# Looping over head pairs outermost, and contracting the mode weights by quarters of d

## The chip, the core and the metric

The kernel runs on one core of a Trainium2 chip. A time is the device time of one execution in microseconds (us). The engines are named as in the profile: PE is TensorE (matmul), PEld its weight loads, DVE is VectorE, ACT is ScalarE, POOL is GpSimd and SP is SyncE. POOL and SP issue the loads and stores (DMA) here. Matmuls leave their results in PSUM; the copy that takes one out to SBUF is called its eviction. The granted clock (PEclk, or the number before the DMA share in a window) is the share of PE's full clock that the profile's record shows.

## The reference, cut to what matters

Eight batches, eight heads, 576 positions, 64 elements per head, so d = 512. A causal attention with a decay that is a difference of cumulative sums is followed by a mixing in frequency space.

```python
scores = q @ k.T / sqrt(64)
cum    = cumsum(log(clip(f, 1e-4, 1)))
scores = where(causal, -1e9, scores + cum[i] - cum[j])
x      = softmax(scores) @ v              # joined to [8, 576, 512]

X  = rfft(x, axis=1)[:, :64]              # 64 modes
Yr = Xr @ w_r - Xi @ w_i                  # w_r, w_i: [64, 512, 512]
Yi = Xr @ w_i + Xi @ w_r
y  = irfft(Y, n=576, axis=1)
u  = x + y
return u + relu(u @ w_ch)                 # w_ch: [512, 512]
```

The weights of the modes are 2 x 64 x 1.05 MB = 134 MB in float32. They are converted to bf16 on their way into SBUF, where they are 67 MB. All of q, k and v is 28 MB in float32, or 14.2 MB in bf16. The transform of x along the sequence treats every column of x by itself, and the contraction with the weights is a sum over d. Both facts are what the change lives on.

## The kernel before

Attention loops over batches, and over the four head pairs of a batch inside. A pair's scores have their 64 head elements on 64 partitions. The decay of a key enters as the bias of the exp, so every tile of 128 keys and every head needs an exp of its own.

```python
pairs = [(b, g) for b in range(B) for g in range(H // 2)]
for i, (b, g) in enumerate(pairs):
    # ... loads of a new batch, transposes of the next pair, AV of the last batch
    emit_qk_pair(b, g, [])

# in emit_qk_pair
for hp in range(2):
    bp = hp * 64
    nc.tensor.matmul(pscore[:Mj, 0:n],
        lhsT=KTs[bp : bp + 64, s0 : s0 + Mj],
        rhs=QTs[bp : bp + 64, s0 + c0 : s0 + c0 + n], start=True, stop=True)
# ...
nc.scalar.activation(et[:Mj, c0 : c0 + n], pss[hp][:Mj, 0:n], ACT.Exp,
                     bias=biasAll[:Mj, jb, bh : bh + 1], scale=scale)
```

AV multiplies the exps with V, which carries a column of ones for the sum of the softmax. After all ten AV groups of a batch, the batch is transformed (`emit_dft_batch`). Only when the last batch is transformed can the contraction with the weights start: a mode takes all 512 rows of d, four matmuls deep in PSUM.

```python
wpool = ctx.enter_context(tc.tile_pool(name="wpool", bufs=6))
# ... all attention ...
for m in range(NM):
    wb = wpool.tile([128, 2, NEB, D], BF16, tag="wb", name="wb")
    nc.gpsimd.dma_start(wb[:, 0], moe_w_r[m].rearrange("(dc p) e -> p dc e", p=128))
    nc.gpsimd.dma_start(wb[:, 1], moe_w_i[m].rearrange("(dc p) e -> p dc e", p=128))
    A = psM.tile([128, 2, NEB, 2 * B], F32, tag="A", name="A")
    for t in range(2):
        for ebx in range(NEB):
            for dc in range(NEB):
                nc.tensor.matmul(A[:, t, ebx, :],
                    lhsT=wb[:, t, dc, ebx * 128 : (ebx + 1) * 128],
                    rhs=_strided(XT[:, dc, 0, m, 0:1], [[1, 2], [NM * 2, B]]),
                    start=(dc == 0), stop=(dc == NEB - 1))
    # ... ACT copies A, DVE forms Yr and Yi ...
    if m % 8 == 3:
        xw_for_batch(m // 8)          # x @ w_ch of one batch, "XW" below
# ... tail: y = irfft, y @ w_ch, u, relu, store: 40 blocks of 128 or 64 rows
```

The softmax here doesn't subtract the row's maximum and nothing guards it: scores larger than these inputs give would overflow.

Of the kernel before, what the change touches and what calls it, by code (L numbers as in the profile page):

```python
# [21 lines left out]
def kernel(  # L24
# [19 lines left out]
    NEB = D // 128  # L44
    BH = B * H
    scale = 1.0 / math.sqrt(Dh)

    const = ctx.enter_context(tc.tile_pool(name="const", bufs=1))
    xpool = ctx.enter_context(tc.tile_pool(name="xpool", bufs=1))
    wpool = ctx.enter_context(tc.tile_pool(name="wpool", bufs=6))  # L50

    x_all = xpool.tile([128, B, NSB, D], BF16, name="x_all")
    XT = xpool.tile([128, NEB, B, NM, 2], BF16, name="XT")
# [4 lines left out]
    masks.make_identity(nc, ident_bf[:])  # L58
    masks.make_identity(nc, ident_f[:])
    masks.make_upper_triangular(nc, trimask[:], val=1.0, diag=True)  # L60

    iota_p_i = const.tile([128, 1], I32, name="iota_p_i")
    nc.gpsimd.iota(iota_p_i[:], pattern=[[0, 1]], base=0, channel_multiplier=1)
    s_i = const.tile([128, NSB], I32, name="s_i")
    nc.gpsimd.iota(s_i[:], pattern=[[128, NSB]], base=0, channel_multiplier=1)
    s_f = const.tile([128, NSB], F32, name="s_f")
    nc.vector.tensor_copy(s_f[:], s_i[:])
    nc.vector.tensor_scalar(s_f[:], s_f[:], float(S - 1), None, ALU.min)
    ones_row = const.tile([1, 128], F32, name="ones_row")
    nc.vector.memset(ones_row[:], 1.0)  # L70
    negpi = const.tile([128, 1], F32, name="negpi")
    nc.vector.memset(negpi[:], -math.pi)

    bas = const.tile([128, NSB, NM, 2], BF16, name="bas")
    BI = const.tile([128, S], BF16, name="BI")
    cumT = const.tile([128, NSB, BH], F32, name="cumT")
    biasAll = const.tile([128, NSB, BH], F32, name="biasAll")
    wch = const.tile([128, NEB, D], BF16, name="wch")

    TWO_PI_OVER_S = 2.0 * math.pi / S  # L80

    with ExitStack() as sctx:
        ps_setup = sctx.enter_context(
            tc.tile_pool(name="ps_setup", bufs=2, space=bass.MemoryType.PSUM)
        )
        ssb = sctx.enter_context(tc.tile_pool(name="setup_sb", bufs=1))

        gem = ssb.tile([128, NSB], F32, name="gem")
        nc.vector.tensor_scalar(gem[:], s_f[:], 432.0, None, ALU.is_ge)
        spl = ssb.tile([128, NSB], F32, name="spl")  # L90
        nc.vector.tensor_scalar(spl[:], s_f[:], 144.0, None, ALU.add)
        sz = ssb.tile([128, NSB], F32, name="sz")
        nc.vector.scalar_tensor_tensor(
            sz[:], gem[:], -float(S), spl[:], ALU.mult, ALU.add
        )
        S0 = ssb.tile([128, NSB], F32, name="S0")
        C0 = ssb.tile([128, NSB], F32, name="C0")
        nc.scalar.activation(
            S0[:], s_f[:], ACT.Sin, bias=negpi[:, :], scale=TWO_PI_OVER_S
        )  # L100
        nc.scalar.activation(
            C0[:], sz[:], ACT.Sin, bias=negpi[:, :], scale=TWO_PI_OVER_S
        )
        Zt = ssb.tile([128, NSB, NM, 2], F32, name="Zt")
        nc.vector.memset(Zt[:, :, 0, 0], 1.0)
        nc.vector.memset(Zt[:, :, 0, 1], 0.0)
        nc.vector.tensor_scalar(Zt[:, :, 1, 0], C0[:], -1.0, None, ALU.mult)
        nc.vector.tensor_copy(Zt[:, :, 1, 1], S0[:])
        wrot = ssb.tile([128, NSB, 2], F32, name="wrot")
        nc.vector.tensor_copy(wrot[:, :, :], Zt[:, :, 1, :])  # L110
        ta = ssb.tile([128, NSB, 32], F32, name="ta")
        tb = ssb.tile([128, NSB, 32], F32, name="tb")
        M = 2
        while M < NM:
            wr = wrot[:, :, 0]
            wi = wrot[:, :, 1]
            t0 = ssb.tile([128, NSB], F32, name="t0")
            t1 = ssb.tile([128, NSB], F32, name="t1")
            nc.vector.tensor_tensor(t0[:], wr, wr, ALU.mult)
            nc.vector.tensor_tensor(t1[:], wi, wi, ALU.mult)  # L120
            t2 = ssb.tile([128, NSB], F32, name="t2")
            nc.vector.tensor_tensor(t2[:], wr, wi, ALU.mult)
            nc.vector.tensor_tensor(wrot[:, :, 0], t0[:], t1[:], ALU.subtract)
            nc.vector.tensor_scalar(wrot[:, :, 1], t2[:], 2.0, None, ALU.mult)
            Are = Zt[:, :, 0:M, 0]
            Aim = Zt[:, :, 0:M, 1]
            wr_b = _strided(wrot[:, :, 0:1], [[2, NSB], [0, M]])
            wi_b = _strided(wrot[:, :, 1:2], [[2, NSB], [0, M]])
            nc.vector.tensor_tensor(ta[:, :, 0:M], Are, wr_b, ALU.mult)
            nc.vector.tensor_tensor(tb[:, :, 0:M], Aim, wi_b, ALU.mult)  # L130
            nc.vector.tensor_tensor(Zt[:, :, M : 2 * M, 0], ta[:, :, 0:M], tb[:, :, 0:M], ALU.subtract)
            nc.vector.tensor_tensor(ta[:, :, 0:M], Are, wi_b, ALU.mult)
            nc.vector.tensor_tensor(tb[:, :, 0:M], Aim, wr_b, ALU.mult)
            nc.vector.tensor_tensor(Zt[:, :, M : 2 * M, 1], ta[:, :, 0:M], tb[:, :, 0:M], ALU.add)
            M *= 2
        nc.vector.tensor_copy(bas[:, :, :, :], Zt[:, :, :, :])
        coef = ssb.tile([128, 1], F32, name="coef")
        nc.vector.memset(coef[:], 2.0 / S)
        nc.vector.memset(coef[0:2, :], 1.0 / S)
        for sc in range(NSB):  # L140
            ns = SBLK[sc]
            bip = ps_setup.tile([128, 128], F32, tag="sps", name="bip")
            nc.tensor.transpose(
                bip[:, :ns],
                Zt[:ns, sc, :, :].rearrange("p m ri -> p (m ri)"),
                ident_f[:ns, :ns],
            )
            nc.vector.tensor_scalar(  # L148
                BI[:, sc * 128 : sc * 128 + ns], bip[:, :ns], coef[:], None, ALU.mult
            )  # L150

        ft = ssb.tile([BH, S], F32, name="ft")
        nc.sync.dma_start(ft[:], f.rearrange("b h s -> (b h) s"))
        lf = ssb.tile([BH, S], F32, name="lf")
        nc.scalar.activation(lf[:], ft[:], ACT.Ln)
        onesS = ssb.tile([BH, S], F32, name="onesS")
        nc.vector.memset(onesS[:], 1.0)
        cum = ssb.tile([BH, S], F32, name="cum")
        nc.vector.tensor_tensor_scan(
            cum[:], onesS[:], lf[:], 0.0, ALU.mult, ALU.add  # L160
        )
        cum_ps = ps_setup.tile([128, NSB, BH], F32, tag="sps2", name="cum_ps")
        for sc in range(NSB):
            ns = SBLK[sc]
            nc.tensor.transpose(
                cum_ps[:ns, sc, :],
                cum[:, sc * 128 : sc * 128 + ns],
                ident_f[:BH, :BH],
            )
        nc.vector.tensor_copy(cumT[:, 0:4, :], cum_ps[:, 0:4, :])  # L170
        nc.vector.tensor_copy(cumT[:64, 4, :], cum_ps[:64, 4, :])
        nc.vector.memset(cumT[64:128, 4, :], 0.0)
        R_ps = ps_setup.tile([128, BH], F32, tag="sps2", name="R_ps")
        nc.tensor.matmul(
            R_ps[:],
            lhsT=ones_row[0:1, :],
            rhs=cumT[0:1, 2, :],
            start=True,
            stop=True,
        )  # L180
        Rb = ssb.tile([128, BH], F32, name="Rb")
        nc.vector.tensor_copy(Rb[:], R_ps[:])
        nc.vector.tensor_tensor(
            biasAll[:, :, :],
            _strided(Rb[:, :], [[0, NSB], [1, BH]]),
            cumT[:, :, :],
            ALU.subtract,
        )

        wch_f = ssb.tile([128, NEB, D], F32, name="wch_f")  # L190
        nc.sync.dma_start(
            wch_f[:], moe_w_ch.rearrange("(eb p) e -> p eb e", p=128)
        )
        nc.vector.tensor_copy(wch[:], wch_f[:])

    with ExitStack() as actx:
        qkbf = actx.enter_context(tc.tile_pool(name="qkbf", bufs=2))
        vapool = actx.enter_context(tc.tile_pool(name="vapool", bufs=2))
        qtkt = actx.enter_context(tc.tile_pool(name="qtkt", bufs=2))
        epool = actx.enter_context(tc.tile_pool(name="epool", bufs=14))  # L200
        psA = actx.enter_context(
            tc.tile_pool(name="psA", bufs=4, space=bass.MemoryType.PSUM)
        )
        psB = actx.enter_context(
            tc.tile_pool(name="psB", bufs=2, space=bass.MemoryType.PSUM)
        )
        psT = actx.enter_context(
# [195 lines left out]
        for it in tails:  # L403
            it()
# [168 lines left out]
```

## Time and profile before

The kernel took 671.9 us (median of 4 runs, 670.98 to 673.73). These are the lines of its page that matter: the span, the busy tenths of PE in 40 slices of 16.8 us, the GB/s that the DMA engines moved in the same slices (bytes as they are written, so bf16 for the weights), and the chain of waits that ended last, by engine and by line.

```profile
span 671.5 us, 10980 instructions
...
PE   0169999999999999999888895222222222225996
...
GB/s 199 185 148 150 36 120 9 98 9 99 8 100 11 97 10 26 1 1 58 202 207 206 207 206 206 206 206 206 206 206 206 206 206 207 206 206 81 134 247 184
...
PE 45%; DMA 44%; DVE 5%; issue 3%; POOL 2%; ACT 0%; SPq 0%; POOLq 0%; DVEq 0%; ACTq 0%
DMA wb<-in_moe_w_r_dram 38%; PE pav L328 14%; PE pscore L293 11%; PE QTp L249 3%; PE KTp L256 3%; DMA wb<-in_moe_w_i_dram 3%; PE px L351 3%; PE pu L507 1%; PE pyw L480 1%; PE pz L529 1%; PE pu L514 1%; PE pz L522 1%; DVE x_all L337 1%; DMA qb<-in_q_dram 1%; PE pxw L435 1%
```

Read the two rows of slices under each other, counted from one. From the 4th to the 19th slice PE is full and the DMA moves 1 to 150 GB/s. From the 20th to the 36th the DMA moves 202 to 207 GB/s in every slice; PE has XW to do in the first five of them, and then two tenths. Then PE is full again. These are three stages with different limits, and they hardly overlap. The Trainium skill, "Perfetto Trace Analysis", section Optimization Strategy, says of such kernels that interleaving the regimes may pay; that is the plan of this change.

| stage | us | limit |
|---|---|---|
| attention | 34 to 310 | PE |
| contraction of the modes, XW in between | 320 to 612 | weight loads |
| tail | 614 to 671 | PE |

The table of windows says the same with numbers. Its columns are the window, its length, busy time and instructions of each engine, the granted clock of PE, the DMA share and the GB/s.

```profile
core 0: us, PE busy (x) PEld busy (x) DVE busy (x) ACT busy (x) POOL busy (x), PEclk, DMA share, GB/s
34.00:310.00 276.00, 262.49 (x1732) 131.67 (x1731) 121.97 (x568) 163.39 (x384) 91.71 (x111) 0.81 0.82 56
320.00:612.00 292.00, 129.73 (x2197) 86.65 (x2195) 38.28 (x146) 38.68 (x99) 80.00 (x108) 0.62 1.24 205
28.00:38.00 10.00, 2.29 (x8) 0.83 (x8) 0.00 (x0) 0.00 (x0) 9.60 (x12) 1.00 2.42 154
```

PE is busy 262.5 of 276 us in the first stage and 130 of 292 us in the second. The third window is a stretch at the start in which only q, k and v are loaded: 154 GB/s, against 206 GB/s for the weights. The rows of q, k and v in HBM are 256 bytes long. What PE waits for in the second stage is in the view of waits (total us, times, longest):

```profile
PE A L456 <- DMA wb<-in_moe_w_i_dram: 85.2, 49, 2.7
PE A L456 <- DMA wb<-in_moe_w_r_dram: 78.0, 48, 2.0
```

That is 163 us of waiting for weights. A stage that is so clearly limited by loads would be free if its loads ran under attention.

PE is not working at its peak in the first stage. This stretch of PE's timeline (start, us, engine, line, operation, shapes) has AV matmuls (`pav`) with 128 rows and a score (`pscore`) with 64 rows.

```profile
260.67 0.25 PE L328 MATMUL pav<-vaug,et_3067 128*64 128x65 bf16 x1
260.73 0.25 PE L328 MATMUL pav<-vaug,et_3068 128*64 128x65 bf16 x1
260.91 0.34 PE L293 MATMUL pscore<-QTs,KTs 64*128 64x192 bf16 x1
261.18 0.26 PE L328 MATMUL pav<-vaug,et_3069 128*64 128x65 bf16 x1
```

The `pav` start 0.06 us apart, but from `pav` to `pscore` it is 0.18 us, and from this score of 192 columns to the next `pav` 0.27 us. The cold clock that the Trainium skill gives ("TensorE: Matmul & The Clock Gate", section Back-to-back issue gap: columns over 1.2 GHz) fits the runs of `pav`; by it 192 columns are 0.16 us, so a change between 64-row and 128-row operands costs some 0.11 us each way, by this estimate.

### The profile page before, as it was taken

How to read it: one execution, taken by the hardware profiler on the slowest of the kernel's cores; microseconds unless marked ns; L12 is line 12 of the kernel's file. 1: busy time of each engine (PE TensorE's matmuls, PEld its weight loads, DVE VectorE, ACT ScalarE, POOL GpSimd, SP SyncE). 2: the span in 40 equal slices, each digit the busy share in tenths (PEclk: the TensorE clock that was granted, in tenths of full speed). 3: DMA queues.
4: the chain of work that ended last, by engine and by line, in shares of the span. 5: the costliest groups of instructions: out<-in, count | busy, mean ns of one | idle time of the engine just before them, and what ended most of it. 6: DMA issues, size and time to landing. Idle time of an engine off the chain costs nothing.

```text
span 671.5 us, 10980 instructions
## 1 busy us (share of the span) xinstructions
PE 457.6 (68%) x4340; PEld 249.0 (37%) x4340; DVE 210.5 (31%) x859; ACT 236.6 (35%) x542; POOL 198.0 (29%) x260
## 2 busy tenths in 40 slices
PE   0169999999999999999888895222222222225996
PEld 0034445454545454545544453222221212123432
DVE  6224444444444444454212120000000010011574
ACT  2046656565656565671232322000000000001553
POOL 5685251515152520003322223232323323210000
PEclk9999999999995555555799877555555555555998
DMA  9999391919191914003999999999999999994375
GB/s 199 185 148 150 36 120 9 98 9 99 8 100 11 97 10 26 1 1 58 202 207 206 207 206 206 206 206 206 206 206 206 206 206 207 206 206 81 134 247 184
DMA packets 186004, 92.62 MB, mean 138 GB/s; under 512 B 115232, under 2 KB 180768, under 8 KB 185952
## 3 DMA queue, kind: packets, MB, share of 16 engines
q0 software_dynamic: 180096, 81.28, 94.6%
q1 hardware_dynamic: 5856, 10.64, 4.6%
q8 instruction: 34, 0.56, 0.3%
q14 instruction: 18, 0.15, 0.1%
HBM read 163.73 MB, written 9.44 MB: 258 GB/s over the span
## 4 chain that ended last, share of the span: by engine, by line
PE 45%; DMA 44%; DVE 5%; issue 3%; POOL 2%; ACT 0%; SPq 0%; POOLq 0%; DVEq 0%; ACTq 0%
DMA wb<-in_moe_w_r_dram 38%; PE pav L328 14%; PE pscore L293 11%; PE QTp L249 3%; PE KTp L256 3%; DMA wb<-in_moe_w_i_dram 3%; PE px L351 3%; PE pu L507 1%; PE pyw L480 1%; PE pz L529 1%; PE pu L514 1%; PE pz L522 1%; DVE x_all L337 1%; DMA qb<-in_q_dram 1%; PE pxw L435 1%
## 5 line engine op out<-in xcount | busy, mean ns | idle before, releaser
L456 PE MATMUL A<-XT,wb 128*128 128x16 bf16 x2048 | 80.6, 192 | 164.0 <-DMA wb<-in_moe_w_i_dram 85.2
L456 PEld LDWEIGHTS <-wb 128*128 128x128 bf16 x2048 | 69.3, 105 | 185.3 <-DMA wb<-in_moe_w_i_dram 94.1
L293 PE MATMUL pscore<-QTs,KTs 64*128 64x320 bf16 (+5 forms) x384 | 119.7, 404 | 0.2
L446 POOL DMA_DIRECT2D wb<-in_moe_w_r_dram x64 | 48.8, 763 | 171.6 <-DMA wb<-in_moe_w_r_dram 95.0
L464 ACT COPY As<-A 128x128 f32<-128x128 f32 x64 | 17.0, 266 | 232.5 <-PE A L456 231.1
L467 DVE TENSOR_TENSOR YT<-As 128x32 bf16<-128x32 f32 x64 | 19.6, 307 | 238.4 <-ACT As L464 238.4
L449 POOL DMA_DIRECT2D wb<-in_moe_w_i_dram x64 | 48.0, 750 | 83.3 <-DMA wb<-in_moe_w_i_dram 83.3
L228 POOL DMA_DIRECT2D vaug<-in_v_dram x40 | 34.0, 868 | 124.7 <-PE pav L328 105.3
L336 DVE RECIPROCAL rcp<-pav 128x4 f32<-128x4 f32 (+1 forms) x80 | 14.6, 183 | 107.2 <-PE pav L328 100.8
L435 PE MATMUL pxw<-wch,xT 128*128 128x512 bf16 (+1 forms) x160 | 47.9, 432 | 0.0
L293 PEld LDWEIGHTS <-KTs 64*128 64x128 bf16 (+1 forms) x384 | 31.1, 107 | 28.2 <-issue 9.9
L220 POOL DMA_DIRECT2D qb<-in_q_dram x40 | 36.2, 905 | 13.2 <-DVE BI L148 12.7
L249 PE MATMUL QTp<-ident_bf,qb 128*128 128x128 bf16 (+1 forms) x160 | 27.7, 288 | 14.8 <-issue 7.9
L224 POOL DMA_DIRECT2D kb<-in_k_dram x40 | 36.3, 908 | 2.0 <-DMA vaug<-in_v_dram 1.0
L442 ACT CAST XW<-pxw 128x512 bf16<-128x512 f32 (+1 forms) x40 | 23.3, 585 | 38.4 <-PE pxw L435 38.1
L337 DVE TENSOR_TENSOR x_all<-pav,rcp 128x256 bf16<-128x256 f32 (+1 forms) x80 | 33.6, 421 | 1.1
L539 DVE SCALAR_TENSOR_TENSOR o_sb<-pz,u_sb 128x512 f32<-128x512 f32 (+1 forms) x40 | 27.3, 689 | 13.9 <-DMA out_dram<-o_sb 5.1
L256 PE MATMUL KTp<-ident_bf,kb 128*128 128x128 bf16 (+1 forms) x160 | 28.6, 289 | 2.1 <-DMA kb<-in_k_dram 2.1
L537 ACT CAST u_sb<-pu 128x512 bf16<-128x512 f32 (+1 forms) x40 | 23.4, 584 | 15.3 <-PE pu L514 12.6
L249 PEld LDWEIGHTS <-qb 128*128 128x128 bf16 (+1 forms) x160 | 14.3, 121 | 29.0 <-issue 19.0
L470 DVE TENSOR_TENSOR YT<-As 128x32 bf16<-128x32 f32 x64 | 22.1, 345 | 0.0
L430 DVE COPY xT<-ptr 128x576 bf16<-128x576 bf16 x32 | 14.6, 462 | 23.4 <-PE ptr L425 23.4
(1386 smaller groups left out, 874.7 us busy)
## 6 DMA issues: line engine op xcount, KB each, us to landing
wb<-in_moe_w_r_dram POOLq DMA_DIRECT2D x64, 512.0 KB, 19.8
wb<-in_moe_w_i_dram POOLq DMA_DIRECT2D x64, 512.0 KB, 20.1
out_dram<-o_sb SPq DMA_DIRECT2D x32, 256.0 KB, 2.0
qb<-in_q_dram POOLq DMA_DIRECT2D x32, 128.0 KB, 4.7
kb<-in_k_dram POOLq DMA_DIRECT2D x32, 128.0 KB, 4.6
vaug<-in_v_dram POOLq DMA_DIRECT2D x32, 128.0 KB, 4.7
wch_f<-in_moe_w_ch_dram SPq DMA_DIRECT2D x1, 1024.0 KB, 5.4
out_dram<-o_sb SPq DMA_DIRECT2D x8, 128.0 KB, 2.3
```

The costliest lines, as they stand in the source:

```text
L220: nc.gpsimd.dma_start(qb[:ns, sc, :, :], q[b, :, sc * 128 : sc * 128 + ns, :].rearrange("h p d -> p h d"),)
L224: nc.gpsimd.dma_start(kb[:ns, sc, :, :], k[b, :, sc * 128 : sc * 128 + ns, :].rearrange("h p d -> p h d"),)
L228: nc.gpsimd.dma_start(vaug[:ns, :, sc, 0:Dh], v[b, :, sc * 128 : sc * 128 + ns, :].rearrange("h p d -> p h d"),)
L249: nc.tensor.transpose(QTp[:, sc * 128 : sc * 128 + ns], qb[:ns, sc, 2 * g : 2 * g + 2, :].rearrange("p h d -> p (h d)"), ident_bf[:ns, :ns],)
L256: nc.tensor.transpose(KTp[:, sc * 128 : sc * 128 + ns], kb[:ns, sc, 2 * g : 2 * g + 2, :].rearrange("p h d -> p (h d)"), ident_bf[:ns, :ns],)
L293: nc.tensor.matmul(pscore[:Mj, 0:n], lhsT=KTs[bp : bp + 64, s0 : s0 + Mj], rhs=QTs[bp : bp + 64, s0 + c0 : s0 + c0 + n], start=True, stop= ...
L328: nc.tensor.matmul(pav[:Ms, hq, :], lhsT=et[:Mj, ccol : ccol + Ms], rhs=vaug[:Mj, h, jb, :], start=(jb == 0), stop=(jb == sb),)
L337: nc.vector.tensor_tensor(x_b[:Ms, sb, hh * 256 : hh * 256 + 256].rearrange("p (h d) -> p h d", h=4), pav[:Ms, :, 0:Dh], _strided(rcp[:Ms, ...
L435: nc.tensor.matmul(pxw[:Ms, :], lhsT=xT[:, eb, sb * 128 : sb * 128 + Ms], rhs=wch[:, eb, :], start=(eb == 0), stop=(eb == NEB - 1),)
L446: nc.gpsimd.dma_start(wb[:, 0, :, :], moe_w_r[m].rearrange("(dc p) e -> p dc e", p=128))
L449: nc.gpsimd.dma_start(wb[:, 1, :, :], moe_w_i[m].rearrange("(dc p) e -> p dc e", p=128))
L456: nc.tensor.matmul(A[:, t, ebx, :], lhsT=wb[:, t, dc, ebx * 128 : (ebx + 1) * 128], rhs=_strided(XT[:, dc, 0, m, 0:1], [[1, 2], [NM * 2, B]]),
```

## The change

The pair of heads becomes the outer loop and the batch the inner one. A pair is 128 of the 512 columns of x. After 8 steps (one pair, all batches) a quarter of the spectrum is complete, and the weights' rows that belong to this quarter can be contracted while attention goes on with the next pair. A weight tile is now 128 rows of d for four modes, real and imaginary, 1.05 MB in bf16: 64 tiles. Two are due per step. The partial sums of the four quarters are added in SBUF, in float32 (`Yacc`).

```diff
-    wpool = ctx.enter_context(tc.tile_pool(name="wpool", bufs=6))
+    wpool = ctx.enter_context(tc.tile_pool(name="wpool", bufs=NRING))      # 11
+    def emit_w_load(n):
+        dc, g = divmod(n, NG)
+        wb = wpool.tile([128, 2, MG, D], BF16, tag="wb", name="wb")
+        for t, src in enumerate((moe_w_r, moe_w_i)):
+            nc.gpsimd.dma_start(wb[:, t, :, :],
+                src[g*MG : (g+1)*MG, dc*128 : (dc+1)*128, :].rearrange("m p e -> p m e"))
+    def emit_modes(n):
+        # ... 32 matmuls of 16 columns into A ...
+        if dc == 0:
+            nc.vector.tensor_copy(ysl, A[:, :, :, :])
+        elif dc < NDC - 1:
+            nc.vector.tensor_tensor(ysl, A[:, :, :, :], ysl, ALU.add)
+        else:
+            # ... writes A + Yacc to YT in bf16, one batch apart: strided ...
-    pairs = [(b, g) for b in range(B) for g in range(H // 2)]
+    steps = [(dc, b) for dc in range(NDC) for b in range(B)]
+    def emit_loads(s):
+        for d, src, eng in ((QKst[s % STG][0], q, nc.gpsimd),
+                            (QKst[s % STG][1], k, nc.gpsimd),
+                            (Vst[s % NV], v, nc.sync)):            # V: float32, by SP
+            # ... one load per head of 512 rows, one of the last 64 rows of both heads
+    # decay in V, and the scores' heads side by side on 128 partitions with zeros
+            nc.vector.tensor_tensor(va, Vt, wdec_of_this_pair, ALU.mult)   # shortened
-                            lhsT=KTs[bp : bp + 64, s0 : s0 + Mj],
+                        lhsT=KTz[s % NK][h][:, jb * 128 : (jb + 1) * 128],
-                            bias=biasAll[:Mj, jb, bh : bh + 1],
+            nc.scalar.activation(E[:, :, piece*512 : piece*512 + w], ps[:, :, 0:w],
+                                 ACT.Exp, scale=scale)             # both heads
+        for s in range(NS + 1):
+            # ... loads of s+3, transposes of s+1, scores of s, AV and DFT of s-1
+            if s > B:
+                for j in range(2):
+                    emit_modes(2 * (s - B - 1) + j)
+                    next_w()
+        # after attention: w_ch is loaded only now (before: at the start)
+        wch = bsb.tile([128, NDC, D], BF16, name="wch")
+        nc.gpsimd.dma_start(wch[:], moe_w_ch.rearrange("(eb p) e -> p eb e", p=128))
+        while nmode < NDC * NG:
+            # ... two tiles of modes, XW of one batch, two weight loads
```

With the decay in V (`wdec` = exp of the old bias), the exp needs no bias, and four exps over both heads replace twelve. The transposed keys are held once per head with zeros in the other head's 64 rows, so that a score uses 128 rows.

## The prediction

It was made from the profile of before alone, with nothing of the change built.

> **What bounds the kernel now.** The page's slices and the table of windows show three stages that hardly overlap.
> (1) Attention, 34 to 310 us: DMA mostly idle (1 to 150 GB/s), PE busy 93 to 99%, about 8.3 us per head pair. PE is slow, not full: 65-column AV matmuls start 54 ns apart in a run (65/1.2 GHz, what the Trainium skill, "TensorE: Matmul & The Clock Gate", Back-to-back issue gap, gives for the cold clock; the trace agrees although the record says 1.0 before 200 us). Every change between 64-row score and 128-row AV operands costs about 0.11 us more (AV to score start 0.17 us instead of 0.05).
> (2) Mode weights, 320 to 612 us: DMA steady at 206 GB/s (bf16 side); PE busy 5 us in 20 between 420 and 600, waiting on weight loads 163 us. Chain: weight loads 41%.
> (3) Tail, 614 to 671 us: PE-bound 512-column matmuls at full clock.
>
> **What changes.** Pair-outer order makes a quarter of the spectrum complete after 8 steps, so weight tiles (64 of 1 MB) stream and are contracted under attention of the next quarters. An 11-deep ring replaces 6. Scores are zero-padded to 128 rows, removing mode switches. Exp loses its bias and covers both heads: 4 per step instead of 12; decay moves to one V multiply (estimate 0.75 us). VectorE sums mode results (estimate 0.4 us per tile). V comes f32 on the SP queue.
>
> **Costs, estimated from trace durations.** Per step cold PE: scores 2.7, transposes 1.1, AV 1.6, DFT 0.5, modes 1.9 (64 x 30 ns): 7.8, with stalls on single PSUM buffers about 10. ACT: three 1,024-element exps 1.04, one small, K evictions 1.4, about 5. DVE about 5. POOL issue about 7. DMA per step: two tiles 2 x 5.08 = 10.2 plus q/k/v 92/32 = 2.9 (14.2 MB at the 154 GB/s of 28 to 38 us), 13.0. The Trainium skill, "DMA: Bandwidth & Descriptors", Why small descriptors are slow, gives 27% overhead at 256 bytes; the trace agrees (154 against 206, 25% less). So the middle becomes DMA-bound.
>
> **Sum.** First 9 steps plus setup about 90 us (weights for the ring and q/k/v fill DMA equally long). Twenty DMA-bound steps at 12.7: to 344. Four steps after the last q/k load, at 9: to 380. Then the last 16 tiles with XW: 8 x 8.5 us, plus about 10 us in which PE waits for the late channel-weight load behind queued tiles: to 458. Tail about 48 us. Total about 506 us. DMA floor: 325 + 92 = 417 us before the tail.
>
> The 290 us weight stage, all on the critical path, disappears as a stage of its own.
>
> **What would show it.** Right: 200+ GB/s from about 20 us to 420 us with no empty slices; chain mostly weight and q/k loads; span per step 12 to 13 us between 100 and 340 us; no 0.11 us switch gaps. Wrong: DMA below 150 GB/s in the middle, with PE the releaser: then steps are latency-bound by single PSUM buffers, at 14 us or more: 540 to 560.
>
> **What would make it wrong.** q/k loads queue behind weights on one in-order queue, and attention starves; weight rows 1 MB apart load slower; PE stays cold in XW (+25 us). Favourable: q/k/v cost less than 92 us, or PE warms: 475.
>
> Predicted: 506 us, 8 in 10 between 472 and 555. Faster by over 2%: 0.96; within 2%: 0.02; slower: 0.02.

## The result, and the profile after

The changed kernel took 541.22 us (median of 4 runs, 539.65 to 543.9). Against before in the same rounds the ratio is 0.8053 (95% interval 0.8024 to 0.8082). Here and below a ratio is the mean time of one kernel's fast runs over that of the other's fast runs of the same rounds, so it is not quite the ratio of the medians that are quoted.

The page of after, same parts as above; a slice is 13.5 us here:

```profile
span 541.8 us, 10785 instructions
...
PE   0626864736765466556554577666651279989996
...
GB/s 153 104 177 186 200 193 189 189 188 200 194 175 196 188 193 193 192 191 192 186 198 198 191 194 189 183 188 195 194 207 206 207 206 204 5 2 87 210 222 182
...
DMA 58%; PE 22%; POOL 6%; DVE 5%; issue 5%; ACT 3%; POOLq 0%; ACTq 0%
DMA wb<-in_moe_w_i_dram 35%; PE pxw L515 7%; DMA stq_119<-in_q_dram 4%; DMA stq_115<-in_q_dram 4%; DMA wb<-in_moe_w_r_dram 4%; DMA stq_117<-in_q_dram 4%; DMA wch<-in_moe_w_ch_dram 4%; POOL wb L78 3%; PE pz L578 2%; DMA stk_122<-in_k_dram 2%; PE pu L570 2%; PE pu L566 2%; PE pz L574 2%; DMA stq_121<-in_q_dram 2%; PE ps L376 2%
```

The empty stretches of the DMA are gone from the 3rd to the 34th slice, and the chain is 58% loads. But the row shows two things that the prediction did not have. In the middle it says 175 to 200 GB/s, not 206. And in slices 35 to 37 the DMA stands nearly still (5, 2, 87 GB/s) while PE runs full: there is still a stage of its own at the end.

To see the pace, take the start of the eviction of the transposed queries (`QTs`), which comes once per step. This table is worked out from the trace.

| what | predicted | after |
|---|---|---|
| tenth step begins | 90 | 89.8 |
| us per step, steps 12 to 30 | 12.7 | 13.9 (109.1 to 359.7 in 18 steps) |
| last q or k load lands | 344 | 383.1 |
| attention ends | 380 | 394 |
| XW ends | 458 | 492 |
| end (profiled run) | 506 | 541.8 |

The windows of after, with the columns as before:

```profile
100.00:340.00 240.00, 143.38 (x2391) 113.62 (x2389) 92.84 (x248) 88.53 (x127) 121.59 (x170) 0.61 1.37 191
395.00:437.70 42.70, 14.26 (x371) 12.64 (x370) 15.75 (x15) 0.04 (x1) 11.93 (x17) 0.50 1.24 206
...
461.00:492.00 31.00, 28.30 (x322) 16.86 (x320) 12.51 (x21) 11.26 (x21) 0.00 (x0) 0.94 0.01 2
```

Between 100 and 340 us the DMA moves 191 GB/s on average. In windows of 1 us between 218 and 262 us it is never idle. From 395 to 437.7 us the DMA is at its full 206 GB/s and PE is busy for 14 of 43 us. From 461 to 492 us it is the other way round: 2 GB/s, and PE 28 of 31 us. Work that PE could have done in the first of these two stretches was done in the second.

What PE waited for (total us, times, longest): weights as before, but a third as long (34.0 us for `w_i` in the line below and 16.9 us for `w_r`), and k loads that stand in line behind the weights. The four k tiles of the ring are listed one by one; the first is shown.

```profile
PE A L97 <- DMA wb<-in_moe_w_i_dram: 34.0, 16, 2.9
PE tp L348 <- DMA stk_116<-in_k_dram: 19.5, 4, 8.1
```

The chain over the seam between attention and the last stage, in order of time (start, us, what):

```profile
374.17 8.89 DMA stk_122<-in_k_dram
...
396.39 20.98 DMA wb<-in_moe_w_r_dram
...
418.15 19.56 DMA wch<-in_moe_w_ch_dram
437.75 7.07 PE pxw L515 x20
```

The load of `wch` is on the chain for 19.56 us. POOL's timeline tells why it takes so long (in brackets: idle time before, and what ended it):

```profile
418.15 0.74 POOL L498 DMA_DIRECT2D wch<-in_moe_w_ch_dram  x1 [2.37 <-DMA wb<-in_moe_w_r_dram]
420.41 0.74 POOL L78 DMA_DIRECT2D wb<-in_moe_w_r_dram  x1 [1.52 <-DMA wb<-in_moe_w_i_dram]
...
435.62 0.74 POOL L78 DMA_DIRECT2D wb<-in_moe_w_r_dram  x1 [2.05 <-DMA wb<-in_moe_w_i_dram]
437.99 0.74 POOL L78 DMA_DIRECT2D wb<-in_moe_w_i_dram  x1 [1.63 <-DMA wch<-in_moe_w_ch_dram]
```

Between the issue of `wch` at 418.15 and the last line lie seven other issues, one every 2.5 us, which is what 512 KB take at 206 GB/s. The eighth issue, the last line, comes 0.3 us after `wch` has landed (418.15 + 19.56) and is released by it. So POOL keeps at most eight loads in flight, and a new load waits behind seven, here for 20 us. The packed trace shows where the eight comes from: POOL's loads signal their landing on eight semaphores, taken in turn, and none of the 313 loads after the first eight starts before the load eight places before it, which had the same semaphore, has landed.

### The profile page after: what moved, and what is told of

It reads as the page before. It is cut to its first block, busy times and chain, and to the rows that moved or that the text cites. A ratio compares the mean times of both kernels' runs of the same rounds, so it can differ in the third digit from the quotient of the medians.

```text
span 541.8 us, 10785 instructions
## 1 busy us (share of the span) xinstructions
PE 341.6 (63%) x4428; PEld 237.6 (44%) x4428; DVE 229.4 (42%) x600; ACT 212.7 (39%) x320; POOL 235.5 (43%) x338
## 4 chain that ended last, share of the span: by engine, by line
DMA 58%; PE 22%; POOL 6%; DVE 5%; issue 5%; ACT 3%; POOLq 0%; ACTq 0%
DMA wb<-in_moe_w_i_dram 35%; PE pxw L515 7%; DMA stq_119<-in_q_dram 4%; DMA stq_115<-in_q_dram 4%; DMA wb<-in_moe_w_r_dram 4%; DMA stq_117<-in_q_dram 4%; DMA wch<-in_moe_w_ch_dram 4%; POOL wb L78 3%; PE pz L578 2%; DMA stk_122<-in_k_dram 2%; PE pu L570 2%; PE pu L566 2%; PE pz L574 2%; DMA stq_121<-in_q_dram 2%; PE ps L376 2%
## 5 line engine op out<-in xcount | busy, mean ns | idle before, releaser
L361 ACT COPY KTz_0_123<-tp 64x640 bf16<-64x640 bf16 x16 | 11.2, 698 | 117.2 <-PE tp L348 117.2
L383 ACT ACTIVATE E_128<-ps 128x1024 bf16<-128x1024 f32 x64 | 51.1, 851 | 6.2 <-PE ps L376 4.8
L383 ACT ACTIVATE E_127<-ps 128x1024 bf16<-128x1024 f32 x64 | 51.1, 851 | 5.0 <-PE ps L376 3.8
L522 ACT CAST XW<-pxw 128x512 bf16<-128x512 f32 x40 | 22.7, 586 | 75.3 <-PE pxw L515 75.3
L361 ACT COPY KTz_0_125<-tp 64x640 bf16<-64x640 bf16 x16 | 11.0, 685 | 84.0 <-PE tp L348 84.0
L515 PE MATMUL pxw<-wch,xT 128*128 128x512 bf16 x160 | 40.4, 408 | 2.7 <-DMA wch<-in_moe_w_ch_dram 1.6
L410 PE MATMUL pav<-va,E_127 128*128 128x65 bf16 x480 | 32.4, 225 | 8.0 <-DVE x_all L419 4.4
L410 PE MATMUL pav<-va,E_128 128*128 128x65 bf16 x480 | 30.6, 221 | 8.8 <-DVE x_all L419 5.6
L97 PE MATMUL A<-XT_4036,wb 128*128 128x16 bf16 x512 | 17.0, 173 | 29.6 <-DMA wb<-in_moe_w_i_dram 14.3
L376 PE MATMUL ps<-QTs,KTz_0_125 128*128 128x512 bf16 (+2 forms) x96 | 28.6, 381 | 6.3 <-ACT E_128 L383 5.1
L97 PE MATMUL A<-XT_1298,wb 128*128 128x16 bf16 x512 | 19.9, 174 | 20.2 <-DMA wb<-in_moe_w_i_dram 11.2
L584 DVE SCALAR_TENSOR_TENSOR uo<-pz,uo 128x512 f32<-128x512 f32 (+1 forms) x40 | 26.8, 687 | 12.7 <-ACT uo L583 12.6
L410 PEld LDWEIGHTS <-E_127 128*128 128x128 bf16 x480 | 26.6, 118 | 12.7 <-DVE x_all L419 6.1
L376 PE MATMUL ps<-QTs,KTz_0_123 128*128 128x512 bf16 (+2 forms) x96 | 27.6, 366 | 7.2 <-ACT E_127 L383 6.6
L419 DVE TENSOR_TENSOR x_all<-pav,rcp 128x384 bf16<-128x384 f32 x64 | 31.1, 486 | 0.8
L410 PEld LDWEIGHTS <-E_128 128*128 128x128 bf16 x480 | 24.9, 116 | 13.3 <-DVE x_all L419 7.9
```

Source lines behind the costliest of these rows:

```text
L97: nc.tensor.matmul(A[:, eb, mi, :], lhsT=wb[:, t, mi, eb * 128 : (eb + 1) * 128], rhs=XT3[:, m, c0 : c0 + 2 * B], start=(t == 0), stop=(t ...
L361: nc.scalar.copy(dst[hs, :], tp[hs, :])
L376: nc.tensor.matmul(ps[:, h, o : o + n], lhsT=KTz[s % NK][h][:, jb * 128 : (jb + 1) * 128], rhs=QT[s][:, jb * 128 + c0 : jb * 128 + c0 + n] ...
L383: nc.scalar.activation(E[:, :, piece * 512 : piece * 512 + w], ps[:, :, 0:w], ACT.Exp, scale=scale,)
L410: nc.tensor.matmul(pav[:, i, h, :], lhsT=E[:, h, c : c + 128], rhs=va[:, jb, h, :], start=(jb == 0), stop=(jb == sb),)
L419: nc.vector.tensor_tensor(x_all[:, b, sbs[0] : sbs[0] + n, dc * 128 : (dc + 1) * 128].rearrange("p c (h d) -> p c h d", h=2), pav[:, 0:n, ...
```

## The experiments

Twelve kernels were run. All gave correct results except one. Times are medians, and ratios are against before in the same rounds. The runs came from several calls, each on one chip; before took 671.87 to 672.58 us (medians) in all of them, so times of different calls may be set side by side.

| run | edit, short | us | ratio to before |
|---|---|---|---|
| after | | 541.22 | 0.8053 |
| rows64 | scores on 64 rows again | 540.41 | 0.8036 |
| half_w | half of the weights not loaded | 403.78 | one run |
| v_bf16 | V by POOL, bf16 | 587.26 | 0.8743 |
| v_f32_pool | V by POOL, float32 | 586.16 | 0.8724 |
| wch_early | w_ch loaded early | 535.5 | 0.7968 |
| wch_order | and XW not behind the modes | 521.01 | 0.7752 |
| before_pad | before, with padded scores only | 604.39 | 0.8979 |
| qk96 | q and k in rows of 1.5 KB | 536.57 | 0.7983 |
| qk96c_order | the same, cheaper evictions, wch_order | 499.06 | 0.7436 |
| qk96c_v_order | and V by POOL, bf16 | 482.63 | 0.7186 |
| qk96c_vf32_order | and V by POOL, float32 | 481.48 | 0.7159 |
| start | qk96c_v_order, first loads reordered | 482.16 | 0.717 |

### Is the middle bound by the DMA, or by a chain through single PSUM buffers?

My theory was that a step takes as long as its bytes. The rival was the one that the prediction itself had named: each step is a chain of PE, ACT and DVE through few PSUM buffers, and takes 14 us by that. The time alone can't decide, as 541 us and 13.9 us per step are about what the prediction had given for the rival (540 to 560, 14 or more). Two runs were made to tell them apart. The first takes half of the weight bytes away and leaves every instruction of PE (its result is wrong: relative error 0.026).

```diff
-        for t, src in enumerate((moe_w_r, moe_w_i)):
+        for t, src in enumerate((moe_w_r,)):
-                        lhsT=wb[:, t, mi, eb * 128 : (eb + 1) * 128],
+                        lhsT=wb[:, 0, mi, eb * 128 : (eb + 1) * 128],
```

> Wrong result on purpose: w_i is never loaded, the matmuls use w_r twice. Same instructions on PE, ACT and DVE, half the weight bytes. DMA theory: the steps between 150 and 370 us shrink from 14.0 us to 9 to 10.5 us (5.1 us of DMA less, then the engines' own work is the limit), total 400 to 450 us. PSUM-chain theory: steps stay near 14 us, total above 520 us.

It took 403.78 us (one run, so no interval; a difference of 137 us needs none). The last 19 steps took 8.8 us each (97.9 to 264.6 us) instead of 13.9. That is 5.1 us less, just what the 1.05 MB taken away need at 206 GB/s, and a little below the 9 to 10.5 us expected. So the chain of engines can run a step in 8.8 us. One thing is not the same, though: PE ran faster too. The AV matmuls of a run start 30 ns apart here and 53 ns apart in after (medians of the middle, worked out from the traces), so a part of the 5.1 us could be PE's. What is left of the rival after that is small: with PE about as slow as in after (53 ns), `qk96c_vf32_order` below, whose loads are cheaper, takes 12.6 us per step. The row of GB/s of `half_w` (slices of 10 us), with the loads over in the 31st slice and the last stage behind them:

```profile
GB/s 161 60 194 170 198 175 144 192 121 129 187 185 197 183 195 196 186 192 184 192 178 208 135 182 187 173 200 207 206 178 52 2 2 2 2 118 233 217 197 181
```

The second run leaves the bytes and makes PE's scores what they were, 64 rows without the zeros.

```diff
-                        lhsT=KTz[s % NK][h][:, jb * 128 : (jb + 1) * 128],
-                        rhs=QT[s][:, jb * 128 + c0 : jb * 128 + c0 + n],
+                        lhsT=KTz[s % NK][h][h * 64 : h * 64 + 64, jb * 128 : (jb + 1) * 128],
+                        rhs=QT[s][h * 64 : h * 64 + 64, jb * 128 + c0 : jb * 128 + c0 + n],
```

> Scores use the 64-row halves of the same K tiles and of Q again, so the switches between 64-row and 128-row operands come back; everything else stays. DMA theory: PE has slack in the middle, 541 within 1.5%, steps still 14.0 us, with gaps of about 0.17 us at the switches. PE theory: 12 switches of 0.11 to 0.2 us per step come on top, 32 x 1.5 to 2.4 us, so 580 us or more.

540.41 us (538.81 to 542.12), no difference that these rounds show. That does not prove that PE has slack, because PE did not get more to do. This is the same window as above, where after had 143.38 us of PE:

```profile
100.00:340.00 240.00, 143.30 (x2383) 110.35 (x2379) 92.46 (x245) 84.87 (x127) 121.53 (x169) 0.54 1.37 192
```

The switches are back, about six per step (not the twelve expected) of 0.14 us each, worked out from the trace. But of 166 scores that follow another score directly, 56 start less than 12 ns after it and run side by side; the padded ones of 64 columns, the shortest, start 28 ns apart. Padding gives back here what it saves. That the middle is bound by loads rests on `half_w`, on the chain and on the DMA that is never idle, not on this run.

### What the zero padding is worth where PE is the limit

If the switches between 64 and 128 rows really cost what the timeline suggested, padding alone must help the kernel before, where attention waits for nothing but PE. This is the kernel before with the scores padded, nothing else.

```diff
-            KTs = qtkt.tile([128, S], BF16, tag="KTs", name="KTs")
+            KTs = KTz[g % 2]          # two tiles, zeros in the other head's rows
-                nc.vector.tensor_copy(KTs[:, :], KTp[:, :])
+                for h in range(2):
+                    hs = slice(h * 64, h * 64 + 64)
+                    nc.vector.tensor_copy(KTs[h][hs, :], KTp[hs, :])
-                            lhsT=KTs[bp : bp + 64, s0 : s0 + Mj],
-                            rhs=QTs[bp : bp + 64, s0 + c0 : s0 + c0 + n],
+                            lhsT=KTs[hp][:, s0 : s0 + Mj],
+                            rhs=QTs[:, s0 + c0 : s0 + c0 + n],
```

> The kernel before with one part of the change alone: scores padded to 128 rows. There PE binds attention, so the part should pay, which it did not in the changed kernel (rows64): 14 to 20 switches per pair at about 0.11 us, 1.5 to 2.2 us less per pair, total 672 - 50 to 70 = 602 to 622 us. If the switch gaps are not what they seem (hidden behind ACT or the AV waits), less than 2%.

604.39 us (601.5 to 609.12), ratio 0.8979 (0.8948 to 0.9009). PE's busy time fell from 457.6 to 378.4 us, and the same slices as before now read:

```profile
PE   0159898979889799998888722222222222227995
...
GB/s 181 164 142 148 177 116 115 26 94 47 72 80 40 40 2 2 99 206 206 206 207 206 206 206 207 206 207 206 206 206 206 206 207 206 206 202 13 208 244 173
```

Attention ends earlier, and the weights' stage, with its 206 GB/s, follows as long as it was. So padding is worth 67 us in the kernel before, as expected, and nothing in the kernel after. But the 67 us are not the price of the switches alone. Compare five transposes of 128 columns, which the edit does not touch, in before and then here:

```profile
224.10 0.78 PE L256 MATMUL KTp<-ident_bf,kb 128*128 128x128 bf16 x5
```

```profile
220.68 0.52 PE L265 MATMUL KTp<-ident_bf,kb 128*128 128x128 bf16 x5
```

In the attention of before they start 106 ns apart, here 55; the AV matmuls of a run start 54 ns apart in before and 34 here (medians, worked out from the traces). So PE ran at about twice the clock in most of this attention. The gaps went too: from `pav` to a score of 192 columns it is 33 ns instead of 176. How the 67 us divide between the gaps and the clock was not tested, nor why the clock rose. The hit does therefore not confirm 0.11 us per switch, and what makes padding worth nothing in after is in part that these gains are not there: in the middle of after PE keeps the slow spacing (53 ns), and a step of `rows64` has six switches where a pair of before has 17.

### The late load of w_ch, and what PE has queued before XW

The seam showed XW starting at 437.75 us, when `wch` landed. The theory was that this load is all that holds XW back. The run allocates `wch` at the start and loads it with the ninth step.

```diff
+    wch = const.tile([128, NDC, D], BF16, name="wch")
+            if s == B:                                   # shortened
+                nc.gpsimd.dma_start(wch[:], moe_w_ch.rearrange("(eb p) e -> p eb e", p=128))
-        wch = bsb.tile([128, NDC, D], BF16, name="wch")
-        nc.gpsimd.dma_start(wch[:], moe_w_ch.rearrange("(eb p) e -> p eb e", p=128))
```

> The channel weights are loaded during step 8 instead of after attention. Theory: XW, which waited until 437.8 us for them, starts at about 397 us and overlaps the last weight loads; the end of the weight stage is then set by the last weight tile (about 461 us) plus the work after it, so total 515 to 522 us. Rival (XW after attention is bound by the PE order and weights anyway): within 1% of 541.

535.5 us (534.37 to 537.93): a miss. Six microseconds came back, not twenty. XW still began only at 428.0 us. The trace of PE shows what stood before it: from 396 us on the matmuls of nine weight tiles, the last four of which wait for their own loads to land. PE works off its instructions in the order in which they are queued (XW waited although `wch` had landed at 107 us), and the queue that the scheduler made had modes first, though the source alternates modes and XW. The theory was incomplete: there are two causes in a row, and taking the first away exposes the second. The next run takes both away. The mode matmuls of a pass may be queued only behind the XW of the pass before.

```diff
-            for _ in range(2):
-                emit_modes(nmode)
-                nmode += 1
+            with tc.issue_after(after.ins) if after else ExitStack():
+                for _ in range(2):
+                    emit_modes(nmode)
+                    nmode += 1
-                emit_xw(nx)
+                after = emit_xw(nx)      # returns its last matmul
```

> As wch_early, and the mode matmuls of the last stage are queued on PE behind the XW of the pass before. wch_early gained only 6 us; theory: its XW still started at 428 us because the PE order put eight tiles of modes, each waiting for its load, ahead of it. With the order fixed XW starts at about 400 us and runs between tiles; PE is done a few us after the last tile (about 458 us), total 512 to 520 us. Rival (something else holds XW): 535 us as in wch_early.

521.01 us (520.23 to 521.72), ratio 0.7752, 1 us above the range that was expected. XW now begins at 401.0 us. The window from 384 to 428 us of the two runs, first with the early load alone:

```profile
384.00:428.00 44.00, 19.61 (x377) 15.88 (x377) 16.99 (x23) 5.78 (x9) 15.86 (x22) 0.54 1.24 206
```

With the order:

```profile
384.00:428.00 44.00, 34.98 (x462) 22.91 (x461) 19.39 (x34) 14.26 (x24) 15.55 (x22) 0.81 1.24 206
```

PE's busy time in these 44 us rises from 19.6 to 35.0 us at the same 206 GB/s. So the seam was worth 20 us: 6 for the load and 14 for the order on top of it (the order without the early load was not run).

### What q, k and V cost on the DMA

A step of 13.9 us holds two weight tiles: 2 x 1.05 MB at 206 GB/s are 10.2 us. What is left, 3.7 us, is q, k and V; the prediction had 2.9 for them. V is the suspect, since it comes in float32 and by SP. The first test changes the type and the queue.

```diff
-        Vst = [stv.tile([128, NSB, 2, Dh + 1], F32, name=f"Vst{i}") for i in range(NV)]
+        Vst = [stv.tile([128, NSB, 2, Dh + 1], BF16, name=f"Vst{i}") for i in range(NV)]
-                (Vst[s % NV], v, nc.sync),
+                (Vst[s % NV], v, nc.gpsimd),
```

> V is loaded as bf16 through the POOL queue instead of as f32 through the SP queue. Theory (DMA-bound middle, V costing about 2.0 us of DMA time per step of 14.0): V falls to about 1.0 us, steps to 13.0 us, total 541 - 32 = about 510 us (505 to 518). Rival (steps bound by the chain through single PSUM buffers): no change, 541 within 1%. Third possibility: POOL issue, with three more loads per step, delays q/k: slower than 541.

587.26 us (585.82 to 589.38), slower than after by 46 us: a clear miss of the theory, with the sign wrong. Only the third possibility, slower through POOL, came true. The second keeps float32 and changes the queue alone (only the last of the lines above).

> V stays f32 but is issued by POOL. It separates the two parts of the V change. If the doubled cost of V comes from the hardware queue of SP (each 256-byte row its own packet), it goes away here too: about 510 us. If it comes from writing 256 bytes of f32 per row instead of 128 of bf16, it stays: about 541 us. The PSUM-chain theory expects 541 us as well.

586.16 us, the same. The windows of 1 us in the middle of `v_bf16` show that the DMA now nearly runs dry:

```profile
223.00:224.00 1.00, 0.20 (x8) 0.11 (x5) 0.42 (x1) 0.00 (x0) 0.80 (x2) 0.50 1.87 118
224.00:225.00 1.00, 0.10 (x2) 0.13 (x3) 0.00 (x0) 0.00 (x0) 1.00 (x2) 0.50 0.69 44
225.00:226.00 1.00, 1.00 (x12) 1.00 (x12) 0.00 (x0) 0.00 (x0) 1.00 (x2) 0.50 0.92 57
```

And POOL's timeline over the same stretch:

```profile
220.89 0.77 POOL L162 DMA_DIRECT2D Vst<-in_v_dram  x1 [2.15 <-DVE Yacc L108]
223.20 0.74 POOL L162 DMA_DIRECT2D Vst<-in_v_dram  x1 [1.53 <-DMA wb<-in_moe_w_i_dram]
...
224.52 0.79 POOL L78 DMA_DIRECT2D wb<-in_moe_w_r_dram  x1
```

With V there are 13 loads per step on POOL, and 9 of them are small. POOL needs 0.6 to 0.8 us to issue any load, and keeps at most eight in flight, as the seam showed. When the eight are all small, they hold too few bytes for the time that the next issues take: the last weight load in flight lands at 222.9 us, then small loads alone are in flight, and the rate falls to 44 GB/s from 224 to 225 us, while the next weight load (224.52) is only being issued. These two runs therefore say nothing about V itself; they say that V on the SP queue was good for something: it kept small loads out of POOL's eight.

To ask about V alone, the number of small loads had to come down first. A batch's q of one pair can be one load if 96 partitions take six successive positions each: two heads, 384 contiguous elements, 1.5 KB of HBM per row instead of 256 bytes. The positions then come out permuted, and the eviction after the transpose must put them back.

```diff
+            for i, src in enumerate((q, k)):
+                nc.gpsimd.dma_start(QKst[s % STG][i][:, :, :],
+                    src[b, 2*dc : 2*dc + 2, :, :].rearrange("h (p c) d -> p h (c d)", p=96))
+                for h in range(2):
+                    for sc in range(6):
+                        nc.tensor.transpose(tp[h*64 : h*64 + 64, sc, :],
+                            src[:, h, sc * Dh : (sc + 1) * Dh], ident_bf[:96, :96])
-                        nc.scalar.copy(dst[hs, :], tp[hs, :])
+                        nc.scalar.copy(
+                            dst[hs, 0:S].rearrange("p (s c) -> p c s", c=6), tp[hs, :, :])
```

> q and k are loaded with one DMA per tensor and step, in 1.5 KB source rows (six positions per partition) instead of 256-byte rows in three DMAs; the order is put right when the transposes are evicted. V as in the change. Theory of DMA cost per row: q/k fall from 1.9 to about 1.4 us per step or a little less, total 541 - 14 to 20 = 521 to 527 us. If small DMAs in the POOL queue (at most about eight loads in flight, counted by DMA and not by bytes) also leave the weights short, the gain is larger. If the PSUM chain binds: no gain, or slower for 14 more PE instructions per step.

536.57 us (535.24 to 537.65): a miss again. The gain on the DMA was eaten by the evictions. These are the groups of the K evictions of after (one of four alike) and of this run (line, engine, operation, shapes, count, then busy us and mean ns, then idle):

```profile
L361 ACT COPY KTz_1_124<-tp 64x640 bf16<-64x640 bf16 x16 | 11.0, 687 | 0.4
```

In qk96:

```profile
L368 ACT COPY KTz<-tp 64x576 bf16<-64x576 bf16 x64 | 132.8, 2075 | 110.5 <-PE tp L353 109.7
```

The copies that write with a stride of six elements take 2,075 ns instead of 687 ns on ACT, and on DVE, for the queries, 2,079 ns instead of 460 ns. With two copies per step on ACT and one on DVE that is 2.8 and 1.6 us more in each step, and slices 8 to 10 of this run's row fell to 129, 56 and 148 GB/s. The remedy is to read with the stride and write in order:

```diff
-                            dst[hs, 0:S].rearrange("p (s c) -> p c s", c=6), tp[hs, :, :])
+                            dst[hs, 0:S].rearrange("p (s c) -> p s c", c=6),
+                            tp[hs, :, :].rearrange("p c s -> p s c"))
```

> qk96 with the order of positions put right in the read of PSUM instead of in the write to SBUF (in qk96 each 576-element eviction with a 12-byte write stride took 2.08 us instead of 0.69, on ACT twice a step, and slices 8 to 10 show DMA at 56 to 148 GB/s behind it), together with wch_order. Theory: evictions return to 0.5 to 0.8 us, the early steps no longer starve DMA, the steps stay at 13.6 us or a little less; total 521 - 12 to 20 = 500 to 509 us. If a strided read of PSUM costs what the strided write cost: 515 us or more.

499.06 us (498.4 to 501.11), 1 us below the expected range, together with the ordered XW: 22 us less than wch_order. Most of that was gained early: the 18th step begins 15 us sooner than in wch_order, and from there a step takes 13.7 us instead of 14.0. The K copies now take 639 ns:

```profile
L370 ACT COPY KTz<-tp 64x576 bf16<-64x576 bf16 x64 | 40.9, 639 | 172.6 <-PE tp L354 171.8
```

Now V can move to POOL without starving it, as there are 9 loads per step, and 5 of them small. First in bf16, then in float32; the edit is that of `v_bf16` and `v_f32_pool`.

> The same with V as bf16 through the POOL queue. With q and k in two DMAs the POOL queue holds nine DMAs per step instead of thirteen (v_bf16). Theory (v_bf16 lost because some eight loads in flight, nine of thirteen small, leave the weights short, and V itself costs half as bf16): no DMA slices below 180 GB/s in the middle, V 1.0 us less per step, total 20 to 32 us below qk96c_order. Rival (any V load in the POOL queue delays the weights by its issue): equal or slower than qk96c_order.

> qk96c_v_order with V staged as f32 again but still through POOL. It takes apart what made V cheap in qk96c_v_order (12.8 us per step against 13.5 in qk96c_order): if the number of source rows and the queue decide, 482 us within 1%; if the bytes written do (256 per row instead of 128), about 499 us as qk96c_order. v_f32_pool could not tell, as its DMA had gaps.

482.63 us (482.34 to 483.54) and 481.48 us (480.84 to 481.99). The first is 16 us below qk96c_order, less than the 20 to 32 expected; the second is where it was expected if the bytes written do not matter. The window from 200 to 300 us in the three runs (columns as before, the last one GB/s), first V by SP in float32 (`qk96c_order`):

```profile
200.00:300.00 100.00, 59.50 (x1030) 46.14 (x1034) 38.23 (x99) 34.52 (x53) 31.27 (x44) 0.62 1.24 200
```

V by POOL in bf16:

```profile
200.00:300.00 100.00, 65.00 (x1047) 50.93 (x1053) 42.96 (x102) 34.86 (x54) 50.55 (x72) 0.55 1.34 200
```

V by POOL in float32:

```profile
200.00:300.00 100.00, 66.99 (x1068) 50.61 (x1066) 43.34 (x103) 35.74 (x56) 50.58 (x72) 0.57 1.24 214
```

V by SP and V by POOL in float32 put the same bytes into SBUF, at 200 and 214 GB/s. From the 18th step on a step took 13.7, 12.8 and 12.6 us in these three runs (181.7 to 305.3 us in nine steps, 169.0 to 296.6 in ten, 169.4 to 295.7 in ten). So the price of V is not the bytes of float32: by POOL, 4.7 MB more written cost nothing. Nor is it the number of packets as such: by POOL, V adds 38,400 packets in bf16 and 4,096 in float32, and both steps are equally long. What is dear is V in float32 rows of 256 bytes issued by SP. These are again 38,400 packets, where the same float32 loads by POOL are 4,096, so the queue and the packets changed together; V in longer rows by SP was not run. The Trainium skill, "DMA: Bandwidth & Descriptors", section Why small descriptors are slow, gives a 27% overhead at 256 bytes; q, k and V by POOL in before agree (154 against 206 GB/s, 25% less). V by SP was dearer than that, about 1 us per step over V by POOL from the 18th step to the 27th; in the whole the float32 runs are 17.6 us apart (499.06 and 481.48), and 16.4 with bf16 by POOL. Why, these runs do not show.

### The start

The last run is `qk96c_v_order` with the masks made before the first loads and a weight tile issued behind each of the first three steps' loads, because the first two slices had only 113 and 105 GB/s.

```diff
         for s in range(STG - 1):
             emit_loads(s)
+            next_w()
-            if s < B:
+            if s < B - 2:
                 next_w()
```

> qk96c_v_order with another order at the start only: the masks are built before the first loads are issued, and a weight tile is put behind each of the first three steps' q/k/v. There the first two slices moved 113 and 105 GB/s and PE waited 12.6 us for the identity built by POOL. Theory (the whole span up to the tail is DMA-bound, so bytes not moved in the first 24 us are paid in full at the end): about 11 us of DMA time regained at most, 472 to 478 us. Rival (the start overlaps something else): 482 us.

482.16 us (481.46 to 483.01): no gain, a miss. These are the rows of GB/s, first without the edit:

```profile
GB/s 113 105 196 196 198 196 201 201 201 201 201 201 201 201 201 202 202 202 201 201 200 200 200 200 201 200 197 196 201 206 206 206 206 207 197 16 191 202 198 197
```

With the edit:

```profile
GB/s 125 195 201 195 198 197 167 190 140 203 206 201 201 201 202 200 201 202 203 202 202 202 200 202 201 201 201 201 201 206 207 206 206 207 195 15 195 200 199 197
```

The 2nd slice rose from 105 to 195, and slices 7 to 9 gave it back, down to 140. A hole opened in the steps between 114.7 and 144.9 us, in which PE waits for a k load:

```profile
PE tp L363 <- DMA stk<-in_k_dram: 53.2, 17, 22.6
```

A ring that fills earlier only stops earlier, and the loads of q and k then stand behind more weights. Bytes that are moved forward count only if nothing later waits for them to be moved.

## Why the prediction was right, and where it was off

**Right: what limits each part.** The stage of 290 us disappeared as such, and the middle is bound by the DMA. `half_w` (8.8 us per step), the chain (58% loads) and steps that became shorter with cheaper loads show it. The first nine steps ended where predicted (89.8 against 90), and the tail took 49 us from the end of XW, against 48.

**Right: the gain is not from faster PE work.** PE's busy time fell by 116 us on the pages, from 457.6 to 341.6, but the 64-row scores cost nothing when put back. The padding was worth 67 us on its own in the kernel before, where it came with a faster clock. It is a case of two improvements that do not add up: 671.9 minus 541.2 is 131 us, and 67 of them could be had without the new loop order.

**Off by about 35 us**, in two terms of the sum.

The first is "92/32 = 2.9" for q, k and V in each step, and with it the pace of 12.7. It measured 13.9, and over the 18 steps that were timed that is 22 us. A quarter of this is a slip in the sum: it costs a step at 13.0 and then counts 12.7. For the rest, I took one rate, 154 GB/s of the loads by POOL in bf16, and applied it to V, which the diff gives to SP in float32. In the runs with V by SP and by POOL, which have long rows for q and k, the difference is 16 to 18 us; in after itself V could not be moved without the loss of `v_f32_pool`. The rest of attention came out 8 us shorter than the sum had it (the two steps before the 18 took 9.7 us each, not 12.7), which the prediction did not foresee, so by luck attention ended only 14 us late. One more step of the prediction was wrong without a price of its own: "four steps after the last q/k load". The last of these loads landed at 383.1 us, one step before the end; the lead of three steps with which they are issued had been used up.

The second is "about 10 us in which PE waits for the late channel-weight load". I had seen that wait coming, but at half its length and as one wait. The stage from the end of attention to the end of XW was to take 78 us (380 to 458) and took 98 (394 to 492). It is two causes: the load behind seven others in flight, and the modes that PE had in front of XW. `wch_early` alone gave back 6 us, with the order 20.

Fourteen and 20 us make 34 of the 35. The experiments agree with this from the other side: the two repairs gave back 20 us (`wch_order` against after) and 16 us (V to POOL, once there were few enough small loads). I add them as an estimate; they were not run together on their own.

**Wrong in the signs to look for.** "200+ GB/s with no empty slices" was to show the theory right. The row says 175 to 200 in the middle and 5, 2 and 87 at the seam. The theory of the middle was right all the same. GB/s falls with the share of short rows in the bytes (154 with q, k and V alone, 206 with weights alone), so idle windows and the step's length were the better sign.

**Open.** Why V's rows cost more when SP issues them. Whether POOL could keep more than eight loads in flight: the eight is the number of semaphores that the program gives them, and no run gave more. How the 67 us of `before_pad` divide between switches and clock. And why the scheduler had put the modes first.

The best version is 481.48 us, ratio 0.7159 (0.7147 to 0.7171): 1.5 KB rows for q and k, V by POOL too, an early w_ch and ordered XW. It beats both kernels; `qk96c_v_order` and `start` are within 1.2 us of it.

## What to carry to other kernels

When two stages with different limits are interleaved, their loads stand in one line: cost each load with the rate of its own queue, row length and type, and count how many small ones stand before a large one. When a stage's limit changes, price each edit anew, since what was worth 67 us before was worth nothing after. And before a gain is put down to what an edit removes, look at the spacing of matmuls that it did not touch, which tells whether PE's clock changed as well. At a seam between stages, look at what the in-order queues (PE's instructions, the loads in flight) hold in front of the work that is ready; taking one blocker away may only show the next.

## What the Trainium skill lacked or had wrong

- "DMA: Bandwidth & Descriptors", section Issuing engines are not separate DMA queues, says that issuing from several engines only saves the sequencer's time, which is usually small. Here moving three loads per step from SP to POOL cost 45 us (541.22 to 586.16, float32 kept), as eight mostly small loads in flight did not keep the DMA busy (44 GB/s in the worst window shown, of `v_bf16`).
- The same page, Issuing engine by pattern, calls the hardware-issued loads generally faster. With few enough loads the opposite was so for V in rows of 256 bytes: 499.06 us by SP, 482.63 and 481.48 by POOL.
- I found no page with the number of loads that POOL keeps in flight. In this kernel it is eight, one for each of the semaphores that its loads take in turn: the eighth issue after `wch` came 0.3 us after `wch` had landed.
- "Advanced Engine Details and Errata", section VectorE Performance Modes, asks unit stride for the mode of two elements per cycle, and does not tell a stride in the read from one in the write. A bf16 copy of 576 elements from PSUM took 460 ns in order, 758 ns with a stride in the read, and 2,079 ns with a stride in the write; on ACT it was 687 (for 640 elements), 639 and 2,075 ns. I found pages that speak of a penalty for strided access, but none with the difference between reading and writing.
- I found no page that gives the price of a change between 64-row and 128-row operands on PE: about 0.11 us each way in before by the estimate above, and 0.14 us in `rows64`. What the switches cost the kernel before in all was not separated from the clock.
- "TensorE: Matmul & The Clock Gate", section Seeing it yourself (the HAM trace caveats there), warns that the clock's record may not be trusted. It is so here: the record of before says full clock up to some 200 us, while 65-column matmuls start 54 ns apart, which is the slow clock's spacing by the same page. This is the record, in tenths of full speed per slice of 16.8 us:

```profile
PEclk9999999999995555555799877555555555555998
```
